# Transposing three more tiles of the last layer on TensorE, adding four residuals on VectorE, with a new order table

## The chip, the core and the metric

The kernel runs on one core of a Trainium2 chip. A core has five engines with a queue each: TensorE (matrix products; PE in the profile, PEld its weight loads), ScalarE (ACT), VectorE (DVE), GpSimd (POOL) and SyncE (SP, which here only issues DMAs). Every engine works its own queue in order, and waits on semaphores for the others. The metric is the device time of one execution, in microseconds; a time for a version is the median of several executions.

## What is computed

A sequence of 2048 tokens with 512 features passes through two layers twice: first a layer A (softmax attention in four segments, with a linear memory carried from one segment to the next), then a layer B (linear attention with softmax feature maps). The weights of both passes are the same. In the text "layer 0" and "layer 1" are the first and the second pass. Layer B matters here:

```python
def _B_ref(x, wqkv, w_phi, wo):
    ...
    phi_q = jnp.concatenate([_softmax(pq, axis=-1), _softmax(-pq, axis=-1)], axis=-1)
    phi_k = jnp.concatenate([_softmax(pk, axis=-1), _softmax(-pk, axis=-1)], axis=-1)
    kv = jnp.einsum('bhsf,bhsd->bhfd', phi_k, v)
    z = jnp.einsum('bhsf->bhf', phi_k)
    num = jnp.einsum('bhqf,bhfd->bhqd', phi_q, kv)
    den = jnp.einsum('bhqf,bhf->bhq', phi_q, z)[..., None] + 1e-06
    o = num / den
    return (lambda x, *d: x.transpose(*d))(o, 0, 2, 1, 3).reshape(B, S, D) @ wo
x = A_x
x = x + _A_ref(_layernorm(x, axis=-1), A_wq, A_wk, A_wv, A_wo, A_beta)
x = x + _B_ref(_layernorm(x, axis=-1), B_wqkv, B_w_phi, B_wo)
x = x + _A_ref(_layernorm(x, axis=-1), A_wq, A_wk, A_wv, A_wo, A_beta)
x = x + _B_ref(_layernorm(x, axis=-1), B_wqkv, B_w_phi, B_wo)
```

`kv` and `z` sum over all tokens, so no query of layer B can be finished before the keys of every token are in. In layer 1 that means: after the last keys, all sixteen query tiles of 128 tokens are finished one after another, and the result is stored.

## The kernel before

**Tiles and stages.** The 2048 tokens are 16 tiles of 128 tokens; four tiles are a segment (layer A) or a query chunk (layer B). The residual stream X stays in on-chip memory for the whole run. Products go to PSUM, which holds four tiles of 1024 columns (slots D0 to D3), shared by everything that TensorE computes: a product must wait until the tile that was last in its slot has been read.

**A query tile of layer B** (`b_query`, from line 1030) goes through these steps. TensorE multiplies the query features by `Rkv` (line 326, called N). For tiles 8 to 15 ScalarE copies this to on-chip memory (line 351, p<-D, 1024 columns). VectorE multiplies by the softmax weights (line 1099). From there two ways lead to the transposed tile oT that the output product needs:

- *by DMA*: VectorE adds the two halves (line 1105), then SyncE issues a DMA transpose (line 364);
- *by TensorE* (keys `("b", L, t)` in `PE_T`): `o_T` lets TensorE multiply both halves by the identity and sum them in PSUM, 16 small products (line 901), then ScalarE or VectorE copies the result out (line 359 or 360). The add of line 1105 falls away, since the sum is made in PSUM.

**The output product** (`out_proj`, line 912; `tproj`; TensorE line 341, D<-WB_o) takes two tiles at once, except for tiles 14 and 15, which go alone (`SOLO`). It is emitted as two halves, each a group of its own in TensorE's queue. The residual is added in one of two ways: for tiles in `RES_PE`, TensorE adds X times the identity to the product (line 341, D<-X,ident) and ScalarE or VectorE copies the sum to X (line 359 or 360); for the others VectorE adds PSUM to X (line 933). In layer 1 a store of the tiles to DRAM follows (line 368, SyncE).

**The order.** The program first lists all 2728 operations with their dependences. A table (`ORDER`, a packed text, read by `place`, line 157) then gives three things: the order in which the operations are emitted, the engine of each, and the buffer slot of each tile. It was made offline by a search. Each engine's queue is the table's order, filtered for that engine, so a queue never overtakes: an instruction whose operands are late holds up everything behind it on its engine. Waits follow from the dependences (`emit`, line 190).

The last part of the queues of the kernel before, unpacked from the table (N13 is the product with `Rkv` of tile 13, T15 the TensorE transpose of tile 15, Wo45a and Wo45b the two halves of the output product of tiles 4 and 5, res the add or copy to X, DT a DMA transpose, st a store):

```
TensorE  Wo89a Wo89b N13 Wo45a N14 Wo45b T15 Wo15a Wo67a Wo15b Wo67b Wo1213a Wo1213b Wo14a Wo14b
ScalarE  copy15 res10/11 Ln Exp copy12 copy13 copy14 evac15 res8/9 res15 res14
VectorE  scale add6 mul12 add12 mul15 mul13 add13 res4/5 mul14 add14 res6/7 res12/13
SyncE    DT4 DT5 st2/3 DT7 DT6 DT12 DT13 st10/11 DT14 st15 st0/1 st4/5 st8/9 st6/7 st12/13 st14
```

Here "scale" is the instruction that completes the softmax weights of tiles 12 to 15 (line 1080).

Of the kernel before, what the change touches and what calls it, by code (L numbers as in the profile page):

```python
# [16 lines left out]
D = 512  # L17
H = 32
# [42 lines left out]
class Tile:  # L61
# [17 lines left out]
    @property  # L79
    def t(self):  # L80
        return self.pool.tensors[self.slot]
# [216 lines left out]
class Kernel:  # L298
# [864 lines left out]
def basep(ap):  # L1163
# [16 lines left out]
        | {("b", 0, t) for t in range(4)} | {("xA", 1, t) for t in range(4)} | {("b", 1, 0), ("b", 1, 15)})  # L1180
RES_PE = {(0, t) for t in (2, 3, 6, 7)} | {(1, t) for t in (2, 3, 6, 7, 8, 9, 10, 11, 12, 13, 14, 15)}
# [8 lines left out]
c-rlE1GHty(q<rit+H*~wr$(CZQHI!vAfVL+cvt(=q?*w|32qd^S%Dxo3-A|nt#^pbMM(ZGb00Ed=dL(d`JKYX#jwsCM1F6Pz!299Y_sHp)OQ{dQcw}6oJan05p__hEN3>K~  # L1190
bm*#h@`Xfu_(5nnMdH4h|AROGpQ;ATJP<f!2@@+CW*z4{f0Yw1aXG586XDC;;i9Jd}hK&;hDLL8t(UAOlo{^H2&pLLo>60`5a6kZ=JET!hYW6>dUyr~xU#LSeWCL*NJK0z;u
2T!OCf6AXjgFdTA1cbEtxAQ{|-QE(Z0z(@#z0r(?igI<sedSMP&0C!+C42GW}JKlwb&>M4N7!1VT&=Vd&9|(uF5Cl2!A$$&5AvLCjT(}OdKzh6ei{Lt>!BEJ6tKcc##(vNSf
5zpo9#+FMTna6)EiQq3Fcu!cBp3tzuqCd6zOW1y!(_Mt{c%3@hqQPHr@(Vu0V^RLK86AC1++uph1edygeUL|^ued_0kYsYScH8sGiJpHI1@7A3&@7~a2V#rj0pG=hT}lUgLg
4E4uV<m8e${jc*u_vU^W!M=g<M;;46rW9dQFZ#EtL_24Ni71YPhGm;v!{Fa|(D9D<9nE5^sZv=ipQP+WpjLGg6xM+tBTj7Gvy_yR{@CwxY&a3n^;r_dQcgQeIS=fZMahTX9n
PJ?++2!F&kv;r&OE@145J@6|ij1_SV7DLTr@oOl88KF3q!ADpW!|@tk$3S?A-#}>`kN2=FmcX}E63gKPjKECrIX*^#Z(tjg!tyvBtKxI2f~&AHRzl?a7>S=^HLQ*+aRy4v44
>ga7>6-%GJb+jP~jAujfWr#*Wx=`gTXKd_kzaQFc&9c4crIoa5PQAF?0iK;#8c5H?bC4%mSO?EzHE2m<N8s)fj}msW!gC?Jx_!g+@3J_d_2VPYdt>%*XXOfr?RM>`%$)3#@~
&a3U3_x;TJt;aCd5NtB$LU_#7Hg=idQp?a8t5~0JUSeSBAZrTl5Nzoq2LD|UQm$;mAlBQ-@A6L+8Y=GS<JLRF~7>I`6U_<Od!MKs$VqV&SOKBrodIup`fHvVKDoD$yBo!f`6
7&o1#22)fijv{?uo;&S@h(hEVYn5($KCh=LvbLLrY)GC^3i*WfI(D>zQV2e4$DvyDoaUeFV>;DlpO0(3LHu)@oTJ4gXtv=Bg@~xH@FQGV`FMWNw6pVLfdf&ML{nbMM<#|IT}
f|s4|Tp<|;ItzQx*9fvQpiYDfW8jw;e*+JiM|AHJdkxR9pM4qQYvs2Y8T)hUpUViRgg)9Dzdq#5)*Or<zfo@P>9I*yK~(Wlgmn$s+Lk8|iG?#IvQ1R`yw*%XgHrxx@T2_~9L
D`_6Jq%Cj?SJ5Xlj$6@bJc#RQJbyulun+g;BX}6s(i%!YLG(3!pi~%4-_sd<P4Ov&=9A=aXf=IF35jVdZJ`acj-u!+eoFy-3?k_$oWoSqkH4dBw4KglZr(u`us^5bowSR>DG  # L1200
!h02<pM3IW_0xG~AN|Ig~n5E-uVLJcc7UjDoockL7}#3?sQHU%^7$i=((0ABGro6+2M@{sBAF7hIf6a&Ioh+4&-t;MVjd58)i#hAyF?0lb@r@<7hZiD(gD#!bAK^Kned&uKX
>l;#N>%4Im5yU=Dn0_k`GwWW!ii8J#c&dTj*I1lDwoSyek7M{W*c`CQ3Fy2eqxF*NobzF=0(Fk78v$z9I<CxHu%JP1i#M8MOAE3%So6E7J$=sbQat1y|F?l9e;Yu8fyU_xUM
Tt2!FXY%%m+SEip2N#{InU)JT%MEi20ln<r~=pL23(s%cq1q0vveA2@FA+hXP~O6&dInT&*Mg1jjQrGn$L~72{+|99G8#NH+-0?iDsOdF3`7pgg)bVoQBfUcbuM1(C7RWU!)
9_k-q2ibdoO7Hm)pA(bv44tB8!8h*$7RZq7$(38$m2oRB}^7QB@6iY?rdSMjI(3$NyUB0d)u9k>;rrYn?!KX5_OnlIB@E+W>j5{1N7YQsBtCwJs`Y(!h`#6OT0@3}Kyqh0(X
32~jQhyf(paiCx!#SJ<O=im(ohy?tWgG70;n=1$uJw<!&!cKrl$z3@U1&ci#B5u)hzD>Qv3$7^k@;<I9_H!lil5308TvF5$uegpVD$ek0E+vYI2I4pz;Oe5ZILk-5jHn?_z)
dPH?$CLzFYeJXE+OtxesP@dQ$0~Ygo?i6C+a66#m`hulocm9O4JoG#6fN<;)#Z$k%%eci*V6Q9OB1xk`MC(dO{H*kvPW>=_#G!<|2+rELw=TBDQ!$3B(1y!U;u75lbW$NyHI
OE|Q7f;v%;aDa2LoBL<6<B9*wrC*c|o5vL$bT;_q|2OcEaigw~Uw--Nh2Qfn2;M}6K$Rmb})FO?z#jV9nZX?o)bfU8CD7uRDqOr&-`ipELyXYjU$Q+`($RKWWPBB1q5k16x?
k0wcJ6u&}6vIR&ahIEj%;FyZ#3RK8F-nXUW5ihTfPdy{@}kHkri)8rhL|a4iOV937$+X`crigN6tl%6o+##sN#Zdt5_833F<Cs}d1AhpBBqK3;uEn|JmqO(iP$EVie=(cv0W
?|&$zl=Ay$f2VyD<3R*N;FhWuP?6zfDy`I%TN){9MIuc)qS$$jEW@rC$GY!)@tF0o(i5PQUK@tycu91v$jP4$har4EYk#UXK4d@Bx%bK<zzB94d?;-okxPK)#6xI8L;5Ld*H
;;J|$>dI^4k+?2S$j73#JSpqR8{)pWDeA~u;<mUWeiEnUT~S{)mS^NWaY~+-PecQGR>p#-;)48HJP^;sMcGg`lIP?r@mjnWO=MH~P+XFiWi#1LR#v}=H=?<`B0q@k@~vngd&  # L1210
_sCis~bK$milmSyh2V*;DqF)zk~oOZJnu<sJD_1WJ-pwv$Tsmn^T!mNG~NOD)^WI!eeNWCwXo)>a`hjx;h<wvu(#Gg(j7R|8~R86kg?*X45=DSwvnWSF#apbVGsrIS(ehD;!
# [72 lines left out]
```

## Time and profile before

| | |
|---|---|
| three runs | 472.95, 474.64 and 475.47 us (median 474.64) |
| the profiled execution, its own time | 472.73 us |
| its span (first to last instruction) | 471.0 us |
| GpSimd busy | 57.4 us (12%) |
| DMA transposes issued by SyncE | 138 (76 p<-p, of attention and query tiles; 54 pX<-p, of normalized tiles; 8 of weights) |
| issue to landing of one, median | 3.0 us (p<-p), 3.3 us (pX<-p) |
| stores of the result | 9, of 256 or 128 KB |
| mean granted TensorE clock | 0.994 of full speed |

How to read the profile: an engine's busy time is the time in which it worked on an instruction. Products are pipelined, so that TensorE's rows overlap and a busy TensorE is not one at its peak. The chain that ended last is followed back from the last instruction: at each step to what released it, or to the instruction before it on its engine. A row of the timeline gives the start, the duration, the engine, the line, the operation with output and inputs, the count, and in brackets the idle time ahead of it with what ended it.

### The profile page before, as it was taken

The numbers are of one execution on the slowest core, as the hardware profiler recorded it, in microseconds if no ns is written. First come the engines' busy times: TensorE is split into PE (matmuls) and PEld (weight loads), VectorE is DVE, ScalarE is ACT, GpSimd is POOL, SyncE is SP. The second block draws the span as 40 slices with busy tenths as digits, with TensorE's granted clock in tenths as the row PEclk, the third lists the DMA queues.
The fourth block names the chain that finished last, engine by engine and source line by source line (L and its number), as shares of the span: only waits on it lengthen the run. The fifth ranks groups of instructions, "written<-read, shape, count | busy, mean of one in ns | idle before, by whom it ended". The sixth has DMA issues, their size and how long they took to land.

```text
span 471.0 us, 25402 instructions
## 1 busy us (share of the span) xinstructions
PE 446.6 (95%) x11753; PEld 299.1 (64%) x11753; DVE 421.5 (90%) x801; ACT 423.8 (90%) x552; POOL 57.4 (12%) x137
## 2 busy tenths in 40 slices
PE   8999899999999999999999999999999999999995
PEld 4566666677667666665556776666677667666552
DVE  6999899999889888989999999998988987998992
ACT  4999999999999997689999999998999999686981
POOL 2312022001011101100420120310110020100000
PEclk9999999999999999999999999999999999999899
DMA  8924534452542031100233454452224104200266
GB/s 256 205 55 76 75 73 99 78 91 27 67 71 43 16 49 31 24 3 14 37 81 59 72 80 55 67 94 48 48 27 61 27 20 65 27 13 3 58 93 191
DMA packets 89388, 30.36 MB, mean 64 GB/s; under 512 B 75954, under 2 KB 89282, under 8 KB 89282
## 3 DMA queue, kind: packets, MB, share of 16 engines
q1 hardware_dynamic: 88450, 28.20, 34.2%
q8 instruction: 92, 1.51, 1.3%
q10 hardware_dynamic: 800, 0.52, 0.4%
q14 instruction: 14, 0.11, 0.1%
q0 software_dynamic: 32, 0.02, 0.0%
HBM read 6.31 MB, written 2.10 MB: 18 GB/s over the span
## 4 chain that ended last, share of the span: by engine, by line
PE 61%; ACT 27%; DVE 6%; DMA 3%; issue 2%; SPq 1%; POOL 0%; DVEq 0%
PE D L341 38%; PE D L326 21%; ACT p L351 15%; ACT pF L351 6%; ACT pE L351 3%; DMA p<-p 2%; PE D L666 2%; DVE X L933 1%; DVE stats L584 1%; ACT pS L351 1%; DMA pX<-p 1%; SPq L364 1%; ACT p L359 1%; ACT X L359 1%; DVE p L878 0%
## 5 line engine op out<-in xcount | busy, mean ns | idle before, releaser
L351 ACT ACTIVATE p<-D 128x1024 bf16<-128x1024 f32 (+1 forms) x224 | 223.0, 1038 | 16.5 <-PE D L341 8.8
L326 PE MATMUL D<-pK,pQ 64*128 64x256 bf16 (+3 forms) x1536 | 115.8, 243 | 5.2 <-ACT pF L351 1.6
L351 ACT ACTIVATE pF<-D 128x896 bf16<-128x896 f32 x128 | 116.8, 939 | 1.8 <-PE D L326 1.5
L326 PEld LDWEIGHTS D<-pK,pQ 64*128 64x128 bf16 x1536 | 55.8, 94 | 43.3 <-ACT p L351 6.3
L326 PE MATMUL D<-pV,pF 64*128 64x34 bf16 x1024 | 75.9, 176 | 1.2 <-ACT pE L351 0.4
L326 PE MATMUL D<-pW,pF 64*128 64x34 bf16 x1024 | 73.3, 176 | 0.0
L592 POOL TENSOR_SCALAR rstd<-mv 128x1 f32<-128x1 f32 x60 | 19.8, 341 | 347.8 <-DVE mv L585 347.5
L326 PEld LDWEIGHTS D<-pV,pF 64*128 64x128 bf16 x1024 | 56.6, 93 | 4.1 <-issue 1.0
L326 PE MATMUL D<-pV,p 64*128 64x34 bf16 x1024 | 53.1, 176 | 1.6 <-issue 1.1
L351 ACT ACTIVATE pE<-D 128x768 bf16<-128x768 f32 x64 | 52.0, 826 | 2.4 <-PE D L326 1.8
L326 PEld LDWEIGHTS D<-pW,pF 64*128 64x128 bf16 x1024 | 53.1, 93 | 1.0
L326 PE MATMUL D<-pW,p 64*128 64x34 bf16 x1024 | 52.1, 176 | 0.0
L326 PEld LDWEIGHTS D<-pV,p 64*128 64x128 bf16 x1024 | 47.2, 93 | 3.6 <-issue 1.2
L326 PEld LDWEIGHTS D<-pW,p 64*128 64x128 bf16 x1024 | 46.0, 93 | 1.4
L326 PE MATMUL D<-tri,two 64*128 64x128 bf16 (+1 forms) x384 | 46.7, 234 | 0.0
L584 DVE BATCH_NORM_STATS2 stats<-X 128x6 f32<-128x512 bf16 x64 | 42.7, 680 | 3.5 <-DMA X<-in_A_x_dram 3.2
L326 PE MATMUL D<-pV,pE 64*128 64x34 bf16 x512 | 45.1, 175 | 0.0
L326 PE MATMUL D<-pW,pE 64*128 64x34 bf16 x512 | 43.2, 175 | 0.0
L980 DVE TENSOR_REDUCE pS<-p 128x64 f32<-128x1024 bf16 (+1 forms) x36 | 38.7, 1092 | 1.2 <-ACT p L351 1.2
L341 PE MATMUL D<-pX,WA_q 64*128 64x512 bf16 x256 | 37.6, 376 | 0.3 <-issue 0.2
L341 PE MATMUL D<-pX,WA_k 64*128 64x512 bf16 x256 | 37.0, 376 | 0.5 <-DVE stats L584 0.5
L341 PE MATMUL D<-WB_k,pX 64*128 64x512 bf16 (+1 forms) x288 | 33.8, 353 | 2.2 <-issue 1.4
(135 smaller groups left out, 998.5 us busy)
## 6 DMA issues: line engine op xcount, KB each, us to landing
pW<-pV SPq DMA_DIRECT2D x16, 136.0 KB, 2.8
out_dram<-X SPq DMA_DIRECT2D x7, 256.0 KB, 2.7
X<-in_A_x_dram SPq DMA_DIRECT2D x3, 512.0 KB, 7.4
pX<-in_B_wqkv_dram SPq DMA_DIRECT2D x3, 512.0 KB, 4.9
p<-p SPq DMA_TRANSPOSE x76, 3.0
pX<-p SPq DMA_TRANSPOSE x54, 3.3
WA_k<-in_A_wk_dram SPq DMA_DIRECT2D x2, 256.0 KB, 6.5
WA_v<-in_A_wv_dram SPq DMA_DIRECT2D x1, 512.0 KB, 8.2
```

Of the source, the lines that this page charges most:

```text
L326: ins = e.matmul(out_ap, lhsT, rhs, start=st, stop=sp, tile_position=(basep(lhsT), basep(out_ap)))
L341: ins = e.matmul(out_ap, lhsT[64 * hf:64 * hf + 64], rhs[64 * hf:64 * hf + 64], start=k == 0 and i == 0, stop=k == 1 and i == len(lists[hf ...
L351: return self.g.op({"act": (dur, lambda e: e.activation(out_ap(), in_ap(), func, scale=scale))}, reads, writes, opens, label=label)
L359: ch = {"act": (n / 1.2 + 51, lambda e: e.activation(out_ap(), in_ap(), ACT.Copy)), "dve": ((340 if fast else n / 0.96 + 65), lambda e: e. ...
L364: return self.g.op({"sp": (1200.0, lambda e: [e.dma_start(out_ap(), in_ap(), transpose=True)])}, reads, writes, opens, kind="d", lat=1450. ...
L584: v(lambda e: e.bn_stats(self.stats[:, t, :], self.X[:, t, :]), 602, [R("X", t)], [R("st", t)], label="bn")
L592: v(lambda e: e.tensor_scalar(rs, self.mv[:, t, 1:2], LN_EPS, None, op0=ALU.add), 170, [R("mv", t)], [R("rstd", t)], eng="pool", label="rstd")
L666: ins = e.matmul(D.t[c0:, r0 * 8:r0 * 8 + n], r[:, c0:], ones(r, n), start=True, stop=True, tile_position=(r0, c0))
L933: self.v(lambda e: e.tensor_tensor(X(), X(), src(), ALU.add), 65 + 512 * n / 0.96, pr + xr, xr, label="res")
L980: fn = lambda e, sgn=sgn, eo=eo, Z=Z, n=n: e.tensor_reduce(Z.t[:, 0:64 * n].rearrange("p (k s h) -> p k s h", k=n, s=2)[:, :, sgn, :], eo( ...
```

## The change

Three sets and the table change; no line of the program does.

```diff
 PE_T = ({("xA", 0, t) for t in range(4)} | {("xB", L, 15) for L in range(2)} | {("a", L, 3, 2, 1) for L in range(2)}
-        | {("b", 0, t) for t in range(4)} | {("xA", 1, t) for t in range(4)} | {("b", 1, 0), ("b", 1, 15)})
-RES_PE = {(0, t) for t in (2, 3, 6, 7)} | {(1, t) for t in (2, 3, 6, 7, 8, 9, 10, 11, 12, 13, 14, 15)}
+        | {("b", 0, t) for t in range(4)} | {("xA", 1, t) for t in range(4)} | {("b", 1, 0)} | {("b", 1, t) for t in (12, 13, 14, 15)})
+RES_PE = {(0, t) for t in (2, 3, 6, 7)} | {(1, t) for t in (2, 3, 6, 7, 8, 9, 10, 11)}
...
 ORDER = """
-c-rlE1GHty(q<rit+H*~wr$(CZQHI!vAfVL+cvt(=q?*w|32qd^S%Dxo3-A|nt#^pbMM(ZGb00Ed=dL(d`JKYX#jwsCM1F6Pz!299Y_sHp)OQ{dQcw}6oJan05p__hEN3>K~
...
+c-rlHWt1I9vSvVXbGKT|%*@Qp%*@Qp%*@Qp!k1XNCq*3EoQJKTWCw#s@ocm?Xlm^JNtg@?Af}vZ&qeSMtl+RMV!iW8Xz4Yq=({A2dY9jNDg(O1XP21P#+X9q=J&r0IEYG(9
...
```

- Tiles 12, 13 and 14 of layer 1 are transposed by TensorE, as tile 15 already was: three adds (line 1105) and three DMA transposes go, three groups of 16 small products (line 901) and three copies out of PSUM come, two on VectorE (tiles 12 and 14) and one on ScalarE (tile 13).
- The residuals of tiles 12 to 15 of layer 1 are added by VectorE (line 933) in place of TensorE's product with the identity and a copy: tiles 12 and 13 in one instruction, 14 and 15 in one each.
- The table is replaced as a whole. The search that made the new one let transposes be issued and land late at random. Both tables hold the same 2728 operations (six of them in their new form). Unpacked, the new table is a local re-sorting of the old one: on TensorE 583 of 1054 operations stand at another rank in the queue, by 14 ranks at most; on ScalarE 230 of 547, by 5 at most; on SyncE 129 of 184, by 33 at most; on VectorE 607 of 792, by up to 73. Twelve operations beside the six move to another engine.

The same part of the queues in the new table:

```
TensorE  Wo89a N12 Wo89b N14 T15 Wo45a T12 Wo45b T13 Wo15a T14 Wo15b Wo1213a Wo67a Wo1213b Wo67b Wo14a Wo14b
ScalarE  copy15 res10/11 Ln Exp copy13 copy12 evac15 copy14 res8/9 evac13 res6/7
VectorE  scale mul15 add6 mul12 mul13 evac12 mul14 evac14 res4/5 res15 res12/13 res14
SyncE    DT4 DT5 st10/11 DT7 DT6 st0/1 st4/5 st8/9 st2/3 st15 st12/13 st6/7 st14
```

Its PSUM slots there: D0 holds N13, T15, T12, Wo15 in turn; D1 N12, Wo45, Wo14; D2 N14, T13, Wo1213; D3 Wo89, T14, Wo67.

In the middle of the run the largest moves are on VectorE. Around 86 to 113 us and 274 to 313 us of the profile before, instructions that prepare later tiles move forward in its queue by 12 to 32 ranks: four of the normalization's statistics (line 584), six single-input operations of layer A's feature map (lines 642 and 643) and four normalizations (line 605).

More of the change, by code (lines that the diff above doesn't have):

```diff
@@ L1194 @@
[L1194 to L1201, printed above, removed]
@@ new lines @@
+jT4KqE*DjiEd=fl|;E3IIVfXbvr)CA0zut)Vm|0Sj%QEwqCQAfY`7=m0gKBBX|lP!KvoCny9VP!lpi8K?w>p)-_)TF?d3LJ_D8wV?`hg?tbON#Oz%g;00^SD+ZAgv{^|x<Pl
+i1wG&@42PUB0(!zD7zx+lHY9{8&<jSxSV#lcVHDhe$1nyi!eG1vcOVPo!rTxEccC}@0DWOG41*}hjX7W-<iRD-5Bk6m><=5@CTxLRuoNysU(AbnAsoJgJn$3VgYhs9(qTW`3
+LBw4ZiDog3Gd(l_z^ZiYwUpELuQ-`1F;PPZ-)Dj6_&vY7zERxBd&r$xEhwj6POMe@F^^U39ubjLML2;8SyRj$H6cMeu8(f6lcIATmygua3b8r4<I{c#RD)B3t|?$hdFQ*7Qk
+$n6Nf-N{28CaBp3=WAwPD;xsVShLm`Zhg)splK7$Wo2Mk36U2rFK$6<*4Gc3awFb{g*T3C)V;W5sF`xpcXF#?8TBJ7C+Xf}+&#5e*6(r9dpub~Kz#rg0IyJ9<B2f^?Iu7}TI
@@ new lines @@
+1$M)g_%pqNUbqUg!E-E%NwGKf!3CgrHIBoDP!e}TF^mV}u`-rIV#X@?8N`B*pg2yzkD&yX$4IPzlduf_h-I-Hmd45WnzBPh+z&4>3U|RTR0*%)6P$(Buqr0O*%%8qV0GMxHL
+xbG!}VAT*I)*aNVpcK;X$~L-+)4awebN?$8X^fyu@gnhg<O}YJ7+{a5El;aTJ8}aSKktI%v`0CorC-;tY&~H&Jt4oQZRA0saE@a4z<vg?J0Uf=Lt`zlPh`pC;2LT#O~D6fMF
+*R3B5)Hr$R)u>lUI2^1fuP+V+=&2b{7qF-SurKW~hl(Lb-?39;^Q9k+t8lj?9^d;n=+|&YBQ%?E-L$EO#&O@4BVSZ|fxu_QzdX2#tiaTf`G8dp$Xz4@TNxkV8TtO>o2NouvU
+nvZC;xl@OyRZnAp*>ifnqX=A43|*}`W%PQ8z@KNxSYz;ZcIj>!bgbo1r{WtLbMl$QgSL!^(g`mVFhYHsjwkErxcVL)8H^_MEh_A4X0%IF@Ay-DTtbp<)$=}l4BoAfuG_S+K*
@@ L1246 @@
+b0Iw*9!b9^ob@zLcJt$n4dXcl}{0`Xi-ssM*h)NMTGgrFg&K-y(D|t!hrr5XzaNXaMxe<8Bb&dhIn~ao*RL_$^jyv$6y(N<zWo6%7X>$=gU8V`h9{UDLi1r%L-{3<YN%zwS)
+i{{gZW|v|@UvH~4I#z#RorAbgF69Ymqea|pbVvQKsI<Q{kz@^%M@d#w#3{MrvF^WcVfc@chI{9Jh+doD%A#MQ5O<E7R5P2Gd8ypVbP1FvL^_wnm0$g9zCjZSg2#t_epMG93U
+V|ng)ZOfAK3ZAuJzM-)If~Dsg8WF@C9B8}|)@v+Y_!WZJa4Eu*#bAJFi1HwXP>>g~Ft#4H{{{M(iBt
 """
```

93 lines of the change are left out of this document (45 added, 48 removed).

## The prediction

> **What bounds the kernel now.** I read the page first, then the busy times by stretch, then the chain and the timeline of the last 30 us.
>
> ```profile
> span 471.0 us, 25402 instructions
> ...
> PE 446.6 (95%) x11753; PEld 299.1 (64%) x11753; DVE 421.5 (90%) x801; ACT 423.8 (90%) x552; POOL 57.4 (12%) x137
> ...
> PE 61%; ACT 27%; DVE 6%; DMA 3%; issue 2%; SPq 1%; POOL 0%; DVEq 0%
> ```
>
> Three engines are near full, and the chain runs over TensorE and ScalarE; DMA and SyncE's queue hold 4% of it. The shares are means over stages, so the stretches come next (columns: length, then busy time of PE, PEld, DVE, ACT, POOL, granted clock, DMA share, GB/s).
>
> ```profile
> 100.00:140.00 40.00, 38.42 (x1132) 27.85 (x1124) 35.54 (x62) 37.88 (x46) 4.03 (x8) 1.00 0.46 63
> 260.00:300.00 40.00, 38.99 (x1156) 27.70 (x1148) 38.00 (x76) 39.32 (x48) 8.77 (x20) 1.00 0.48 70
> 457.90:463.10 5.20, 3.66 (x57) 1.99 (x49) 3.05 (x4) 2.31 (x4) 0.00 (x0) 1.00 0.39 71
> 463.10:467.30 4.20, 3.95 (x40) 1.69 (x40) 1.64 (x2) 0.05 (x1) 0.00 (x0) 1.00 0.86 248
> 467.30:471.00 3.70, 0.00 (x0) 0.00 (x0) 0.00 (x0) 0.55 (x1) 0.00 (x0) 0.74 0.74 250
> ```
>
> In the middle ScalarE and TensorE have almost nothing left: 0.68 us idle of 40 on ScalarE from 260 on. The tail is different: from 457.9 on no engine is full, and from 467.3 on only the last copy and the stores remain. The chain names what holds it.
>
> ```profile
> 457.94 0.59 DVE X L933
> 458.53 4.06 DMA p<-p
> 462.59 0.53 issue
> 463.12 1.27 PE D L341 x10
> ...
> 467.25 0.60 ACT X L359
> ```
>
> A DMA transpose of 4.06 us, then four halves of output products, then one copy. The transpose waits in SyncE's queue, the products of tiles 12 and 13 wait for it, and that of 14 follows.
>
> **The tail, part by part.** These rows of the timeline carry the costs.
>
> ```profile
> 442.03 0.69 DVE L360 CAST p<-D 128x512 bf16<-128x512 f32 x1
> ...
> 453.35 0.65 ACT L351 ACTIVATE pS<-pS 128x128 f32<-128x128 f32 x2
> ...
> 455.08 6.85 SPq L364 DMA_TRANSPOSE p<-p  x4
> ...
> 456.86 1.04 PE L341 MATMUL D<-WB_o,p 64*128 64x512 bf16 x8
> 457.07 1.02 ACT L351 ACTIVATE p<-D 128x1024 bf16<-128x1024 f32 x1 [0.51 <-PE D L326]
> 457.73 0.41 PE L901 MATMUL D<-ident,p 64*128 64x64 bf16 x16
> 458.17 0.60 ACT L359 ACTIVATE p<-D 128x512 bf16<-128x512 f32 x1
> 459.08 0.68 DVE L1099 TENSOR_TENSOR p<-p,pS 128x1024 bf16<-128x1024 bf16 x1
> 459.80 0.42 DVE L1105 TENSOR_TENSOR p<-p 128x512 bf16<-128x512 bf16 x1
> 460.57 0.60 PE L341 MATMUL D<-WB_o,p 64*128 64x256 bf16 x8
> 462.94 1.19 SPq L364 DMA_TRANSPOSE p<-p  x1
> 463.12 0.39 PE L341 MATMUL D<-X,ident 64*128 64x512 bf16 x2 [0.87 <-DMA p<-p]
> 463.34 1.04 PE L341 MATMUL D<-WB_o,p 64*128 64x512 bf16 x8
> 464.19 4.16 SPq L368 DMA_DIRECT2D out_dram<-X  x7
> 465.70 0.28 PE L341 MATMUL D<-X,ident 64*128 64x256 bf16 x2
> ```
>
> *Removed:* on VectorE three adds of 0.42 us; on SyncE three transposes, of 1.19 us of issue each (one here alone; four in a row took 6.85); on TensorE the identity products of the residuals, which make 1.26 us of a half (463.12 to 464.38) where 1.04 is enough without, and add some 0.1 to the 0.60 of a lone tile's half. *Added:* on TensorE three transposes of 0.41 us; on VectorE two copies of 0.69, on ScalarE one of 0.60. *Exchanged:* VectorE's residual adds cost what its copies did for two tiles; for one tile the row is
>
> ```profile
> L933 DVE TENSOR_TENSOR X<-X,D 128x512 bf16<-128x512 bf16 x6 | 4.0, 683 | 0.4 <-PE D L341 0.4
> ```
>
> against ScalarE's 0.60. For one tile the way from the multiply to oT was 0.42 for the add, 1.19 of issue and a landing 3 us after it; it becomes 0.41 and 0.60 to 0.69. But the new chain passes through PSUM slots and through VectorE's queue, so I follow it through the new table's queues instead of subtracting. I start both from the same point: ScalarE ends its last Exp of the weights at 454.00 (453.35 and 0.65); up to there the two tables issue the same ScalarE and VectorE work.
>
> 1. ScalarE: copy13, copy12, evac15, copy14: three copies of 1.02 and one of 0.60, 3.66 us at most, some 0.1 less at each overlap of neighbours. copy14 ends about 457.45.
> 2. VectorE: mul12 needs copy12 (ends 455.9): 455.95 to 456.65 (0.68); mul13 to 457.3. TensorE's T12 needs slot D0, which evac15 frees at 456.5; it ends about 457.25. So evac12 runs to 458.05 and mul14 to 458.75.
> 3. T14 (slot D3, free once res8/9 has ended at 458.45) runs 458.85 to 459.25; evac14, 0.69, ends at 460.0. What is behind evac14 in VectorE's queue (res4/5, res15) is not urgent yet, except that Wo14 needs the slot of Wo45, freed by res4/5 at 461.2, before its turn comes.
> 4. Wo67 uses T14's slot, so it cannot start ahead of 460.05. From there stand five halves: 1.26, 1.04, 1.26, 0.60, 0.60. End to end they make 4.76; in groups that interleave, starts stand closer by the product's last 0.16 (457.73 lies 0.17 before the end of 456.86 and 1.04), 4.1. I take 4.6, since each half waits for its first. The last ends at 464.65.
> 5. VectorE adds tile 14, 0.68: 465.4. Before, the last copy ended at 467.85 (467.25 and 0.60).
>
> From there to the end of the span before is 3.15 us (issue and landing of the last store); I leave it. Ahead of it SyncE issues seven stores behind res4/5 (461.2), as many as the seven that took 4.16 us before from 464.19; they begin 3 us earlier, so they don't bind. The tail gains 467.85 - 465.4 = **2.45 us**. Bounds: if all engines had to work end to end and VectorE's two evacuations came a product (1.04) late, 1.0; if the evacuations don't hold the slots and Wo67 starts with T13 done (458.9), 3.6.
>
> **The rest of the table.** The new order is a local re-sorting, so stages stay where they are. The waits of TensorE that it could remove are few:
>
> ```profile
> PE D L341 <- issue: 1.9, 3, 1.4
> PE D L341 <- DMA p<-p: 1.5, 2, 0.9
> ...
> PE D L341 <- DMA pX<-p: 0.5, 1, 0.5
> ```
>
> The 0.9 belongs to the tail. The others, 0.6 and 0.5, and the 1.4 of "issue", ahead of a product whose operand is a late normalized tile, make 2.5 us, the most that earlier transposes give directly. The other bound is a loss through VectorE's new order (below). Transposes that are ready sooner stand ahead of others in SyncE's queue at the place of the 0.5; at the others little changes. I take a gain of 0.5.
>
> **Sum.** 472.73 - 2.45 - 0.5 = 469.8 for an execution like the profiled one. That one was the fastest of the four known; their mean is 473.95, 1.2 above it, the median of the three runs 1.9 above. I add 1.2 here and to each rival: **471.0 us**, its own range 468.5 to 473.5.
>
> **Rival 1: the gain is eaten by a slow clock.** The granted clock fell once ahead of the tail:
>
> ```profile
> 434.00:436.00 2.00, 1.30 (x50) 1.05 (x52) 1.82 (x6) 1.56 (x4) 0.00 (x0) 0.74 0.00 0
> 436.00:438.00 2.00, 2.00 (x37) 1.06 (x35) 2.00 (x4) 1.83 (x4) 0.00 (x0) 0.50 0.04 8
> 438.00:440.00 2.00, 2.00 (x88) 1.55 (x84) 1.56 (x5) 1.66 (x2) 0.00 (x0) 0.91 0.32 66
> ...
> 435.75 1.91 PE L341 MATMUL D<-pX,WB_q 64*128 64x512 bf16 x8
> ```
>
> Eight products took 1.91 us instead of 1.04 there, behind a stretch of many small products and waits. The lost clock is 2 times (0.26 + 0.50 + 0.09), 1.7 us of full-speed work. The new tail has such a stretch from 455.3 to 459.5: four transposes of 64 columns, with waits for copies between them. A dip behind it would fall on the last halves: 469.8 + 1.7 + 1.2 = 472.7, and with the slots' lower bound (1.0 instead of 2.45) 474.2; I name 473.6. Against it: from 457.9 to 463.1 TensorE was busy 3.66 of 5.20 us, and its clock stayed at 1.00.
>
> The Trainium skill, "TensorE: Matmul & The Clock Gate", Part 1, has a rule for it: the array runs at half clock after a window of about 3.4 us without enough activity and at full clock after a busy one, with windows that run freely. The rows agree with half clock (0.50) and about its length; by this rule the dip before may vanish or move in any execution, which is no reason to expect it more after.
>
> **Rival 2: the whole order gains.** The 2.5 us of waits go, and what stood behind them moves up: 472.73 - 2.45 - 2.5 + 1.2 = 469.0. For it: DMA and SPq are 4% of the chain. Against it: TensorE was busy with other work during most of those links.
>
> **Rival 3: slower, by VectorE's order.** Place: layer 0 at 86 to 113 us and layer 1 at 274 to 313, where the new table brings preparations for later tiles ahead of evacuations that TensorE's slots and ScalarE's inputs wait for. The rows:
>
> ```profile
> L584 DVE BATCH_NORM_STATS2 stats<-X 128x6 f32<-128x512 bf16 x64 | 42.7, 680 | 3.5 <-DMA X<-in_A_x_dram 3.2
> ...
> L605 DVE TENSOR_SCALAR p<-X,mv,rstd 128x512 bf16<-128x512 bf16 x64 | 24.6, 400 | 0.6 <-POOL rstd L594 0.5
> ...
> L642 DVE TENSOR_SCALAR p<-pK 128x1024 bf16<-128x1024 bf16 x12 | 5.0, 419 | 0.0
> ```
>
> Price: 4 x 0.68 + 4 x 0.40 + 6 x 0.42 = 6.8 us, if none is absorbed: 472.73 - 2.45 + 6.8 + 1.2 = 478.3. It decides from 5.3 us on, where it outweighs 2.45 + 0.5 by the 2.4 us that make half a per cent. For it: VectorE has 2.0 us idle of 40 from 260 on, ScalarE 0.68. Against it: from 100 to 140 VectorE has 4.5 us idle, and other instructions move back by as much, so that most evacuations keep their rank.
>
> **That the change doesn't do what it says** (a table made against random lateness that meets the chip's lateness no better) is inside the forecast: it rests on the tail alone.
>
> **How the numbers follow.** Half a per cent, 2.4 us, is about what a measurement of this kernel can tell from no change; it puts the borders at 472.3 and 477.0. The forecast has 0.50 (0.42 faster, 0.08 same), rival 1 0.20 (0.01, 0.18, 0.01), rival 2 0.12 (all faster), rival 3 0.18 (0.00, 0.03, 0.15). Together: faster 0.55, same 0.29, slower 0.16. The range: down to rival 2 with the tail's better bound and without the 1.2 (469.0 - 1.15 - 1.2 = 466.6), up to rival 3's price, 478.3.
>
> **What would show it.** Right: VectorE's last row is a residual add of 128x512 that ends 5 to 6 us before the span's end; no DMA p<-p in the last 12 us of the chain; TensorE's idle time between the last Exp of the weights and its own last product falls below 2 us. Step 3 is wrong if T14 starts well after mul14's end. Rival 1 shows as a granted clock under 0.9 in the last 12 us, rival 3 as ScalarE busy less than 37.5 of 40 us around 100 to 140 or 260 to 300 with VectorE as releaser. The forecast fails if the stretch up to that Exp (454.00 us before) changes by more than 2.5 us.

## The result, and the profile after

The changed kernel took 469.21 us in the median of four executions (468.53 to 471.16), the kernel before 475.06 us beside it: a ratio of 0.989, 95% interval 0.984 to 0.994. Twelve more executions, taken later beside 27 of the kernel before, gave 0.993 (0.990 to 0.996). The first ratio makes the gain 5.3 us (3.0 to 7.5), the second 3.4 us (1.9 to 4.8). The profiled execution took 468.75 us, its span 466.7 us (472.73 and 471.0 before).

The page of the profile of the kernel after gives the span, the busy times, the shares of the chain, and the median landing of query and attention transposes.

```profile
span 466.7 us, 25467 instructions
...
PE 446.3 (96%) x11789; PEld 298.7 (64%) x11789; DVE 420.2 (90%) x800; ACT 423.3 (91%) x552; POOL 56.2 (12%) x138
...
PE 57%; ACT 34%; DVE 4%; DMA 3%; issue 2%; POOL 1%; SPq 0%; DVEq 0%
...
p<-p SPq DMA_TRANSPOSE x73, 3.1
```

The engines do as much work as before (TensorE 446.6 us then, 446.3 now) in a span that is 4.3 us shorter, so what went is waiting. The two stretches in the middle, in the columns of the windows shown before:

```profile
100.00:140.00 40.00, 38.39 (x1142) 27.45 (x1138) 35.25 (x63) 38.58 (x47) 2.98 (x8) 1.00 0.27 46
260.00:300.00 40.00, 38.85 (x1200) 28.06 (x1196) 37.90 (x76) 39.14 (x48) 7.40 (x17) 1.00 0.46 70
```

ScalarE stays at 38.6 and 39.1 of 40 us: it is not starved by VectorE's new order, and rival 3 is out. The rows of the tail, from the timeline:

```profile
451.66 0.66 ACT L351 ACTIVATE pS<-pS 128x128 f32<-128x128 f32 x2
451.80 0.69 SPq L368 DMA_DIRECT2D out_dram<-X  x1
...
455.11 1.04 PE L341 MATMUL D<-WB_o,p 64*128 64x512 bf16 x8 [0.92 <-DMA p<-p]
...
455.97 0.41 PE L901 MATMUL D<-ident,p 64*128 64x64 bf16 x16
...
456.43 0.69 DVE L360 CAST p<-D 128x512 bf16<-128x512 f32 x1 [0.96 <-PE D L901]
...
457.03 0.68 DVE L1099 TENSOR_TENSOR p<-p,pS 128x1024 bf16<-128x1024 bf16 x1
...
457.77 0.41 PE L901 MATMUL D<-ident,p 64*128 64x64 bf16 x16
...
458.22 0.69 DVE L360 CAST p<-D 128x512 bf16<-128x512 f32 x1 [0.51 <-PE D L901]
...
461.47 1.22 DVE L933 TENSOR_TENSOR X<-X,D 128x1024 bf16<-128x1024 bf16 x1 [0.83 <-PE D L341]
...
463.66 0.69 DVE L933 TENSOR_TENSOR X<-X,D 128x512 bf16<-128x512 bf16 x1 [0.97 <-PE D L341]
```

The last Exp of the weights ends at 452.32 (454.00 before), the last residual at 464.35 (467.85), the span at 466.7 (471.0). So by these two executions 1.7 us were gained ahead of the tail, 1.8 in it, and 0.8 behind the last residual. The chain of waits says what the new tail waits for:

```profile
446.12 1.83 ACT p L351 x2
449.62 5.41 DMA p<-p
455.11 1.04 PE D L341 x8
458.18 4.78 PE D L341 x52
```

The transposes of tiles 12 to 14 have left the chain, and an older one stands in it, that of tile 5: 5.41 us from its issue to the product that needs it, for which TensorE idles 0.92 us. The transpose of tile 12 by TensorE (455.97) stands behind that product in the queue.

Were these three pieces the change's doing? Two traces can't tell. The experiments take the pieces apart, and each leaves a further trace of a part of the old or the new order.

### The profile page after: what moved, and what is told of

The parts are those of the page before. It is cut to its first block, busy times and chain, and to the rows that moved or that the text cites. A ratio compares the mean times of both kernels' runs of the same rounds, so it can differ in the third digit from the quotient of the medians.

```text
span 466.7 us, 25467 instructions
## 1 busy us (share of the span) xinstructions
PE 446.3 (96%) x11789; PEld 298.7 (64%) x11789; DVE 420.2 (90%) x800; ACT 423.3 (91%) x552; POOL 56.2 (12%) x138
## 4 chain that ended last, share of the span: by engine, by line
PE 57%; ACT 34%; DVE 4%; DMA 3%; issue 2%; POOL 1%; SPq 0%; DVEq 0%
PE D L341 36%; PE D L326 18%; ACT p L351 18%; ACT pF L351 9%; ACT pE L351 4%; DMA p<-p 2%; PE D L666 2%; DMA pX<-p 1%; ACT pS L351 1%; DVE X L933 1%; ACT p L359 1%; DVE p L795 1%; DVE pK L360 0%; POOL rstd L594 0%; ACT X L359 0%
## 5 line engine op out<-in xcount | busy, mean ns | idle before, releaser
L326 PE MATMUL D<-pK,pQ 64*128 64x256 bf16 (+3 forms) x1536 | 114.2, 243 | 5.1 <-ACT p L351 1.3
L592 POOL TENSOR_SCALAR rstd<-mv 128x1 f32<-128x1 f32 x60 | 16.2, 275 | 351.8 <-DVE mv L585 351.7
L980 DVE TENSOR_REDUCE pS<-p 128x64 f32<-128x1024 bf16 (+1 forms) x36 | 38.6, 1090 | 0.3 <-ACT p L351 0.2
L594 POOL TENSOR_TENSOR rstd<-rstd,mhalf 128x1 f32<-128x1 f32 x60 | 37.9, 639 | 2.4
L933 DVE TENSOR_TENSOR X<-X,D 128x1024 bf16<-128x1024 bf16 (+1 forms) x30 | 32.1, 1074 | 6.4 <-PE D L341 6.2
```

Of the source, the lines that this page charges most:

```text
L326: ins = e.matmul(out_ap, lhsT, rhs, start=st, stop=sp, tile_position=(basep(lhsT), basep(out_ap)))
L592: v(lambda e: e.tensor_scalar(rs, self.mv[:, t, 1:2], LN_EPS, None, op0=ALU.add), 170, [R("mv", t)], [R("rstd", t)], eng="pool", label="rstd")
L594: v(lambda e: e.tensor_tensor(rs, rs, self.mhalf[:], ALU.pow), 540, [R("rstd", t), R("mhalf")], [R("rstd", t)], eng="pool", label="rstd")
L933: self.v(lambda e: e.tensor_tensor(X(), X(), src(), ALU.add), 65 + 512 * n / 0.96, pr + xr, xr, label="res")
L980: fn = lambda e, sgn=sgn, eo=eo, Z=Z, n=n: e.tensor_reduce(Z.t[:, 0:64 * n].rearrange("p (k s h) -> p k s h", k=n, s=2)[:, :, sgn, :], eo( ...
```

## The experiments

### The tail alone, and the rest of the table alone

The two tables agree on the set of operations that come first at several places, so they can be cut there: at position 2655 of 2728 (about 450 us), and at position 1300 (about 216 us). Each part keeps its own order, engines and buffers.

```diff
 tail_only
-order = new[0:2655] + new[2655:2728]
+order = old[0:2655] + new[2655:2728]
 bulk_only
-order = old[0:2655] + old[2655:2728]
+order = new[0:2655] + old[2655:2728]
```

> The first 2655 of the 2728 instructions in the order, engines and buffers of the kernel before, the last 73 (from 450 us on) in those of the kernel after, with its three TensorE transposes and its VectorE residual adds. The tail's term of the prediction (2.45 us): 2.45 us below the kernel before. What the two traces show of the tail (1.8 us up to the last residual add, 0.8 us from there to the end): 1.8 to 2.6 us below it. The rival, that the gain came from the rest of the table: within 0.5 us of the kernel before.

> The other half of the same cut: the first 2655 instructions as in the kernel after, the last 73 as in the kernel before (three DMA transposes, residuals of tiles 12 to 15 by TensorE). The prediction's term for the rest of the table: 0.5 us below the kernel before. What the two traces show at the last Exp of the weights: 1.7 us below it, and up to 3 us if the clock dips as briefly as in the trace of before (3.4 us instead of 6.8 us at half clock). The rival, that the table's body is worth nothing and the traces differ by the clock alone: within 0.4 us.

The tail alone: 471.47 us, ratio to before 0.9935 (0.9907 to 0.9963), which is 3.1 us (1.8 to 4.4). The rest alone: 472.88 us, ratio 0.9969 (0.9941 to 0.9996), 1.5 us (0.2 to 2.8). So by the middle values the tail carries two thirds of the gain, and the two rivals "nothing from the tail" and "nothing from the rest" fall, the second narrowly. tail_only holds the new forms and the new order of the last 73 operations together; of these the residuals alone are taken apart below, so what the three transposes give without the new order is not measured. The tail in tail_only:

```profile
454.43 0.64 ACT L351 ACTIVATE pS<-pS 128x128 f32<-128x128 f32 x2
...
457.04 1.04 PE L341 MATMUL D<-WB_o,p 64*128 64x512 bf16 x8 [0.23 <-ACT p L351]
...
460.14 0.69 DVE L360 CAST p<-D 128x512 bf16<-128x512 f32 x1 [0.51 <-PE D L901]
...
465.58 0.69 DVE L933 TENSOR_TENSOR X<-X,D 128x512 bf16<-128x512 bf16 x1 [0.97 <-PE D L341]
```

From the end of the Exp (455.07) to the last residual (466.27) it takes 11.20 us, 0.8 less than the same operations in the kernel after: the wait at tile 5 is 0.23 us here instead of 0.92.

### The two halves of the rest

```diff
 first_half
+order = new[0:1300] + old[1300:2728]
 second_half
+order = old[0:1300] + new[1300:2655] + old[2655:2728]
```

> The first 1300 instructions (to 216 us) in the order of the kernel after, the rest as in the kernel before. From two traces of the old body (before, tail_only) and four of the new one (after, bulk_only, res_pe, store_behind), all in one execution each: at 216 us the new one stands at 0.6 to 1.8 us, mean 1.1, ahead of the trace of before, but 0.3 more ahead of tail_only. If the new order gains there: 1 to 1.4 us below the kernel before. If the executions differ by chance alone: within 0.4 us.

> The middle part, instructions 1301 to 2655 (216 to 450 us), in the order of the kernel after, the first 1300 and the last 73 as in the kernel before. In the six traces the middle part up to 415 us is 0.7 to 1.3 us shorter in the new order than in before and tail_only, and the clock's dip then takes back 0.4 to 0.8 us (6.8 us at half clock in all four of the new order, 3.4 us in both of the old): 0.2 to 0.9 us below the kernel before. If the dip costs what the clock record says, half of 3.4 us more: 0.5 us above it.

first_half took 473.33 us, ratio 0.9989 (0.9956 to 1.0021); second_half 472.83 us, ratio 0.9973 (0.9944 to 1.0001). What the rest of the table gives, it gives after 216 us, some 1.3 us, at the edge of what can be told from nothing; the 1 to 1.4 us that the traces promised for the first half did not come. The traces side by side show how far one of them can mislead, in us from the span's start (the end of the first 2473 of the 2728 operations, the same set in both orders; the end of the Exp; and, as the tail, the time from there to the last residual):

```
                order up to 450 / tail   first 2473   Exp's end   tail
before          old / old                  415.4       454.0      13.85
tail_only       old / new                  415.7       455.1      11.20
after           new / new                  412.4       452.3      12.03
after_again     new / new                  414.6       454.8      12.01
bulk_only       new / old                  413.8       453.9      12.98
res_pe          new / new, residuals       413.9       453.9      13.00
store_behind    new / new, store moved     413.8       453.5      11.69
```

after_again is the kernel after, run again; it and the last two are told of below. One body of operations, run five times, ends its first 2473 anywhere from 412.4 to 414.6. The trace of after was the most fortunate of them. The means (415.5 old, 413.7 new) differ by 1.9 us; at the end of the Exp 0.9 of it is left (454.5 and 453.7). The section on the clock shows where the rest goes. The old tail takes 12.6 to 13.9 us in four traces (second_half 12.60, first_half 13.72, and two above), the new one 11.2 to 12.0 in four (without res_pe): 1.6 us between the means, just below the interval of the times (1.8 to 4.4).

The pieces behind the last residual go by chance and not by the tail: from it to the span's end stand 3.1 us in before, 3.4 in first_half and 2.3 in bulk_only with the old tail, 2.4 in after, 2.6 in tail_only and 3.7 in fill_light (below) with the new one.

### The residuals put back on TensorE

```diff
-RES_PE = {...} | {(1, t) for t in (2, 3, 6, 7, 8, 9, 10, 11)}
+RES_PE = {...} | {(1, t) for t in (2, 3, 6, 7, 8, 9, 10, 11, 12, 13, 14, 15)}
```

> The kernel after with the residuals of tiles 12 to 15 of layer B put back on TensorE as products with the identity; their last step is a copy on the same engine at the same place of the order. If TensorE sets the end of the tail, each of the four tiles costs it 0.21 us (distance from the first identity product to the first product that follows it, 448.12 to 448.33 in the trace of after): 0.85 us above the kernel after. If the chain of VectorE and ScalarE sets the end: within 0.3 us of it.

The time was 471.48 us, ratio to before 0.9936 (0.9913 to 0.9959), against 0.9929 (0.9899 to 0.9959) for the kernel after: too close for the times to settle 0.85 us. The trace does it by rows (the last one is the copy that stands in the place of the VectorE add):

```profile
459.01 0.27 PE L341 MATMUL D<-X,ident 64*128 64x256 bf16 x2
459.12 0.60 PE L341 MATMUL D<-WB_o,p 64*128 64x256 bf16 x8
...
463.58 0.38 PE L341 MATMUL D<-X,ident 64*128 64x512 bf16 x2
...
463.80 1.03 PE L341 MATMUL D<-WB_o,p 64*128 64x512 bf16 x8
...
466.20 0.69 DVE L360 CAST X<-D 128x512 bf16<-128x512 f32 x1 [1.19 <-PE D L341]
```

Each identity product of a lone tile's half pushes the next product back by 0.11 us (459.01 to 459.12), that of a pair's half by 0.22; four and two of them make 0.88 us. The tail is 13.00 us instead of 12.03, 0.97 more, of which 0.12 is the wait at tile 5 (1.04 instead of 0.92). From there on TensorE sets the end of the new tail, and by these rows the residual adds are worth their 0.85 us: about half of the 1.6 us that the rows show for the tail, a quarter of the 3.1 us of the times.

### The store moved behind the transposes

```diff
-SyncE  DT4 DT5 st10/11 DT7 DT6 st0/1 ...
+SyncE  DT4 DT5 DT7 DT6 st10/11 st0/1 ...
```

> The kernel after with one store (tiles 10 and 11) moved in SyncE's queue from between the transposes of tiles 5 and 7 to behind that of tile 6. If the store's traffic slows the transpose of tile 5 (5.4 us from issue to landing, where the transposes of its kind have a median of 3.1): that landing falls to 3 to 4 us, TensorE's wait of 0.92 us at 455.1 goes, and the end comes 0.4 to 0.9 us earlier (transposing tile 12 then waits for VectorE's product, which ends 0.5 us before it is transposed now). If the transpose is late by itself: the wait stays at 0.9 us and the time within 0.3 us of the kernel after.

The time was 470.77 us, ratio 0.9915 (0.9884 to 0.9946). TensorE's wait at tile 5 came to 0.59 us, neither 0 nor 0.9, and the landing to 5.1 us; with the store in its old place it had been 5.4 (after), 5.4 (after_again), 5.5 (res_pe) and 4.1 (tail_only). In the three kernels with filling, below, TensorE's wait is 0.1 us (and ends with ScalarE, not with the transpose), with the store in its old place (two) and moved (one). The store is at most a small part of what makes it late. Narrow windows of the DMA view of the kernel after, from tile 5's issue at 449.62 on, show another part (columns of a queue: packets, MB, share of the 16 DMA engines' time; of an issue: median landing):

```profile
q1 hardware_dynamic: 533, 0.13, 48.6%
q8 instruction: 1, 0.02, 7.3%
...
p<-p SPq DMA_TRANSPOSE x1, 5.4
...
q1 hardware_dynamic: 494, 0.12, 78.2%
q14 instruction: 1, 0.01, 5.3%
```

The two windows lie at 449.6 to 450.9 and 450.9 to 452.9. In each starts one packet of a queue that the profile names "instruction": it takes 7.3% of 16 x 1.3, 1.5 us, and 5.3% of 16 x 2.0, 1.7 us. The packets of tile 5's transpose follow these two. Of its 512 packets of 256 bytes 472 have started by 451.6; none starts then until 452.1, when the first instruction packet ends (450.59 to 452.11), and 34 go one after another; the last six start from 453.18 on, when the second ends (451.50 to 453.19). So a part of the transpose waits behind each. The landing at 455.02 still comes 1.6 us behind its last packet, where that of tile 7 comes 0.5 us behind; this part is not explained. Over the records of eight traces, transposes counted by how many such packets (8 or 16 KB) overlap the time from 0.3 to 2.4 us behind their issue:

```
packets   transposes   issue to landing, us: 10%   median   90%
   0          285                            2.41    2.45   2.67
   1          727                            2.43    3.45   4.27
   2           62                            2.98    4.06   4.74
```

So the lateness of a transpose goes with these packets. That they load the program itself is read from the queue's name. The table is a relation in records and not an experiment: moving the loads was not tried.

### Every transpose made late

The new table was searched with transposes that issue and land late. If that made it tolerant, the kernels should move apart when all transposes are late.

```diff
 late_before, late_after (def tr)
-[e.dma_start(out_ap(), in_ap(), transpose=True)]
+[e.dma_start(self.scr[...], self.inp["A_beta"][None, 0:2]), e.dma_start(out_ap(), in_ap(), transpose=True)]
```

> The kernel before with every one of its 138 DMA transposes made late: once its input is ready, SyncE first issues a load of 4 bytes into a cell that nothing reads, then the transpose, and the consumer waits for both. With a delay of 0.65 us each (the issue of one plain transfer on SyncE in the tail takes 0.4 to 0.7 us) the transposes whose time from issue to first use leaves less than that over a landing of 3.1 us add up to 3.2 us in the trace of before, with 1 us to 6.9 us. Both theories: 2 to 8 us above the kernel before.

> The same delay in front of each of the 135 DMA transposes of the kernel after. If the new order tolerates late transposes better: by the same sum 1.6 us (delay of 0.65 us) or 4.6 us (1 us), so it loses 1.6 to 2.3 us less than the kernel before loses, and the distance between the two grows from some 4.5 to 6 to 7 us. The rival, that the orders are equally tolerant and the difference is the tail's: both lose the same within 0.7 us.

late_before took 493.1 us, ratio to before 1.039 (1.034 to 1.044), late_after 486.1 us, ratio to before 1.025 (1.020 to 1.030). Both lose much more than expected, 18.4 us (3.87% of 474.7) and 15.6 (2.48% and the 0.81% by which after lies below before, its two ratios weighted by executions). SyncE's queue in late_after points at why:

```profile
457.00 0.42 SPq L365 DMA_DIRECT2D scr<-in_A_beta_dram  x1
457.47 1.81 SPq L366 DMA_TRANSPOSE p<-p  x1
459.38 0.36 SPq L365 DMA_DIRECT2D scr<-in_A_beta_dram  x1
459.79 1.19 SPq L366 DMA_TRANSPOSE p<-p  x1
```

Each small load takes 0.41 to 0.47 us of the queue up to the next transpose, and the transposes come in groups, so the delays of a group add up; the sum over single slacks left that out, which would explain the miss. The distance between the two came to 7.0 us (some 3 us to either side by the two intervals), and the traces tell where it lies. At the Exp's end late_before stands at 474.2 and late_after at 471.7: 2.5 us apart, 19.6 and 18.0 us behind the means of their bodies. The rest lies in the tail, 15.65 us in late_before and 11.20 in late_after. With nearly equal losses up to the Exp (at the end of the first 1300 operations late_after even stood 10.7 us behind the trace of before, late_before 6.1), a greater tolerance of the table's body is not shown. The tail is more tolerant: late_before's is 1.8 us longer than the longest undelayed one, with TensorE idle four times for 3.8 us together, and late_after's is as short as tail_only's, without three of the late links.

### The clock

All seven traces of the list above show a stretch at half clock ahead of the tail. In the kernel after (length, then busy time of PE, PEld, DVE, ACT, POOL, granted clock, DMA share, GB/s):

```profile
430.00:432.00 2.00, 1.46 (x90) 1.35 (x92) 1.23 (x6) 1.56 (x5) 0.00 (x0) 0.91 0.05 8
432.00:434.00 2.00, 1.38 (x62) 1.13 (x56) 1.97 (x3) 1.15 (x3) 0.00 (x0) 0.50 0.00 0
434.00:436.00 2.00, 1.54 (x75) 1.54 (x77) 1.62 (x6) 2.00 (x5) 0.00 (x0) 0.50 0.12 24
436.00:438.00 2.00, 2.00 (x22) 0.61 (x16) 2.00 (x7) 2.00 (x4) 0.00 (x0) 0.50 0.45 92
438.00:440.00 2.00, 1.93 (x32) 0.94 (x32) 2.00 (x6) 1.18 (x6) 0.00 (x0) 0.88 0.55 97
```

The clock lost is 2 x (0.09 + 0.50 + 0.50 + 0.50 + 0.12) = 3.4 us, so 6.8 us at half speed; in before it was 3.4 us long. The other four traces of the new body have 6.8 us too, tail_only with the old one has 3.4; second_half, new from 216 us on, has 6.8, and first_half, old there, none. The executions that left no trace agree: the mean granted clock is 0.990 over bulk_only's and 0.994 over those of the kernel before beside it. Here the 1.9 us of the body shrink to 0.9: from the first 2473 operations to the Exp's end the two traces of the old body need 38.6 and 39.4 us, the five of the new 39.7 to 40.3. The test is to give TensorE work there; the edit is that of fill_light.

```diff
+FILL = {(1, 0, 0, 1): 2, (1, 2, 1, 1): 4, (1, 1, 1, 1): 6}
...
-for tt in range(4) for gg in range(2) for hf in range(2)],
+for tt in range(4) for gg in range(2) for hf in range(2)] +
+[(ZQ.t[:, hf * 512 + 256:hf * 512 + 512], self.ident[64 * hf:64 * hf + 64, :], self.WB["q"][64 * hf:64 * hf + 64, 0, 0:256], True, True)
+ for _ in range(FILL.get((L, c, gp, sgn), 0)) for hf in range(2)],
```

> The kernel after, unchanged, for a comparison on the chip of the next two runs and a further execution of its trace. By the two halves measured apart (ratio 0.9935 for the tail, 0.9969 for the rest) the whole stands at 0.990; by the first four executions at 0.989. If those four were favoured by chance: 0.992 or above.

> The kernel after with 12 pairs of products added on TensorE (64 rows, 256 columns, 0.107 us a pair; they write PSUM columns that nothing reads) where it idles between small products in layer B's last part: 2 pairs ahead of the idle 0.27 us at 430.1, 4 ahead of 0.41 us at 431.5, 6 ahead of 0.72 us at 434.4. They lie in idle time, so by themselves they cost 0 to 0.2 us. If the clock dips because TensorE does little work there: one of the two stretches of 3.4 us at half clock goes, or both, and the time falls by 0.5 to 1.5 us against the kernel after. If the dip comes whatever TensorE does: 6.8 us at half clock as in all five traces of this body, and 0 to 0.5 us slower.

> The same with 30 pairs (3.2 us of TensorE work, beside all twelve groups of small products), of which about 1.6 us fits into idle time. If the dip follows the amount of work: both stretches at half clock go, which gives 1.0 to 1.5 us, and up to 1.6 us of added work takes that back: within 0.6 us of the kernel after, with a clock record at 1.0 from 420 to 445 us. If the dip comes whatever TensorE does: 1.5 to 3 us slower, with 6.8 us at half clock.

> fill_light and store_behind together: the 12 pairs of products in idle time and the store of tiles 10 and 11 behind the transpose of tile 6. If both gains hold, 1.2 us (the means of fill_light and after_again, 470.06 and 471.27) and 0.3 us (TensorE's wait at tile 5, 0.92 us in after, 0.59 us in store_behind): a ratio of 0.987 to 0.990 to the kernel before, and no clock below full speed between 420 and 445 us in the trace. If fill_light's gain was chance: 0.992 to 0.993, as after_again. If the store has nothing to do with tile 5's landing, TensorE's wait there lies anywhere from 0.2 to 1.0 us, as in the traces with and without the move so far.

The same windows in fill_heavy:

```profile
430.00:432.00 2.00, 1.99 (x92) 1.77 (x88) 1.12 (x4) 1.50 (x3) 0.00 (x0) 1.00 0.00 0
432.00:434.00 2.00, 1.50 (x74) 1.34 (x75) 1.31 (x4) 1.46 (x3) 0.00 (x0) 1.00 0.04 8
434.00:436.00 2.00, 1.62 (x74) 1.36 (x68) 1.97 (x4) 1.50 (x4) 0.00 (x0) 1.00 0.00 0
436.00:438.00 2.00, 1.78 (x58) 1.13 (x58) 2.00 (x8) 1.46 (x3) 0.00 (x0) 1.00 0.41 86
```

The dip is gone in all three filled traces, and the mean granted clock over the executions goes from 0.991 (after_again) to 0.996 (fill_light) and 0.999 (fill_heavy): the dip follows the work.

The 14 traces tell which measure of work (a product's columns are the last number of its shape: 512 in 64x512). All lengths in their clock records, but for the last one of a trace, are whole multiples of 3.413 us (3.41, 6.83, 27.3, 211.6 and 430.1 among them). On the grid of that step, 17 windows at full clock are followed by half clock; TensorE was busy 17 to 87% of them, with products of 1,152 to 6,672 columns in all. Of the 1,864 that kept full clock some were busy only 50%, and all but 12 had more columns than that, the 12 from 5,504 on. Half clock went on behind windows of 3,200 to 6,400 columns and ended behind 6,528 or more. So the columns decide, with a border at some 5,500 to 6,700, and not the busy time. The long dip has two such windows in a row, in after with 4,032 and 3,488 columns; before has 3,200 and then 6,848.

The times gain little. after_again: 471.09 us, ratio 0.9929 (0.9899 to 0.9959), which by what was expected means that the first four executions were favoured by chance, though 0.990 lies inside the interval; fill_light 469.99, 0.9898 (0.9864 to 0.9932); fill_heavy 471.14, 0.992 (0.9891 to 0.9948), its added products having eaten what the clock gave. fill_store, with the light filling and the moved store, came to 472.16, 0.9939 (0.9913 to 0.9966), above both ranges expected, and its executions had clocks from 0.988 to 0.998. The light filling leaves windows of 5,816 (fill_store) and 6,912 columns (fill_light), at the border, so it may keep the clock up only in some executions; the heavy one leaves none under 9,088. The mean clock can't show this by itself, for it counts other places: fill_light's own trace has 0.994 without a dip ahead of the tail, from 3.4 us at half clock near 216 us (tail_only and first_half have that one too) and 2.4 us behind TensorE's last product. So fill_light's gain over the kernel after, 1.1 us of median, did not come back, and no version here is shown to beat the kernel after. Over some 210 executions of these kernels (without the late ones), a line with a level for each puts the price at 0.39 us (standard error 0.07) for each us of lost clock, so that the longer dip, 1.7 us of lost clock more, costs an estimated 0.7 us of the 1.0 us that the stretch is longer. The traces without a dip bear it out: from the first 2473 operations to the Exp's end fill_light and fill_store need 39.3 and 39.1 us where the five of the new body need 40.0 in the mean (fill_heavy, with its added products, 40.6).

## Why the prediction was right

**The place and the size.** The forecast had the tail as what gains, by 2.45 us, and the rest of the table by 0.5. Measured apart they are 3.1 us (1.8 to 4.4) and 1.5 us (0.2 to 2.8); the tail's term lies inside its interval, the other inside but near its edge. The forecast was 471.0 us; the two samples have medians of 469.21 and 471.09. That the second lies so near is in part luck: as a gain over the mean of 473.95 from which it started the forecast was 2.95 us, and the two samples have 5.9 and 3.6 between their medians.

**The tail, step by step.** The 2.45 us took the old tail from one trace, whose 13.85 us are the longest of four (13.3 in the mean); the rows of all traces make the gain 1.6 us. Steps 1 to 5 make 11.4 us from the end of the Exp to that of the last add (465.4 - 454.0). tail_only and all three filled kernels took 11.20, within 0.2. The kernel after took 12.03, and the step that failed there is the second: the transpose of tile 12 was to wait for its slot and end 3.25 us behind the Exp (mul12's end at 456.65 and the 0.41 of a transpose make 3.06). It ended 4.06 behind it (456.38), since the first half of tiles 4 and 5 stands ahead of it in TensorE's queue and waited 0.92 us for tile 5's DMA transpose. The prediction followed VectorE's and ScalarE's queues through the tail, and took the DMA transposes that remained as landed. Step 3 held: the transpose of tile 14 starts at 457.77, right behind VectorE's product for it (457.03 and 0.68), and its copy ends at 458.91, 6.6 behind the Exp where 6.0 were worked out; the difference comes from step 2.

**Behind the last residual** the prediction left 3.15 us unchanged. The 0.8 us that after's trace shows less lie within the scatter of 2.2 to 3.7 us over all traces, old and new tails alike.

**The rest of the table** was the mis-sized term: 0.5 taken, 1.5 measured. In the traces the new body is 1.9 us ahead at 415 us, and half of that goes in the longer dip, which leaves 0.9. That the waits removed are those that the prediction listed (2.5 us in its rival 2) is not shown: up to there TensorE's idle time ended by a DMA falls from 1.3 us (two traces of the old body) to 0.6 (five of the new), and that ended by VectorE, which the prediction feared would grow, from 4.0 to 3.1. The latter falls in first_half too (2.7), whose time hardly moved. So the cause of this part stays open.

**Rival 1** had the right mechanism in the wrong place. The new tail never dipped while TensorE worked, but the dip ahead of it grew from 3.4 to 6.8 us. The prediction looked for new small products only from 455 us on, and not at how the new order places those of the query chunks ahead. In before, windows of 2 us with many products lie at 432 to 436 us (128 and 50, with 42 and 28 in the two ahead of them); in after at 428 to 436 (72, 90, 62 and 75). **Rival 3** did not occur: ScalarE's busy time in its two stretches is 38.6 and 39.1 us, above the 37.5 that would have shown it.

**The marks.** Two of the signs did not come. VectorE's last row is a residual add of 128x512, but it ends 2.35 us before the span's end and not 5 to 6: the 5.6 us (471.0 - 465.4) were counted to the end of the span before, which was to move as well. And a DMA transpose p<-p does reach into the chain's last 12 us, tile 5's (449.62 to 455.03 of 466.7), where none was to stand. The others came: TensorE's idle time behind the Exp was 0.92 us and nothing else above 0.1, under the 2 us named. The stretch up to the Exp changed by 1.7 us, under the 2.5 that would have ended the forecast.

## What to carry to other kernels

When a link is taken off the end of a chain, look at once for the next late operand in the same queue, here an older transpose that nobody had waited for; it decides how much of the gain arrives. A pair of traces of two versions holds a microsecond or two of chance at every milestone, so cut the change in two and measure the parts, and lay the traces of equal parts beside each other, before giving a piece of the difference a cause. Gathering small products into one longer stretch can cost clock: in these traces it took back half of what the new order had gained ahead of it.

## What the runs showed of the hardware

- **DMA transposes are late where packets of the queue "instruction" run.** In the 466.7 us of the kernel after, of 25,467 instructions, 92 such packets of 16 KB and some of 8 KB run, those of 16 KB for about 1.1 us each (1.4% of 16 x 466.7 us, over 92). A transpose that meets none lands in 2.45 us, one that meets two in 4.06 (medians), and at tile 5 in 5.4. This is a relation; only for tile 5 was it followed packet by packet, and there some 1.1 us of the landing stay unexplained.
- **A busy TensorE can lose its clock.** In the kernel after it was busy 2.7 of the 3.4 us from 428.2 on and never idle for more than 0.41 us in a row, mostly with products of 8 and 64 columns, and was set to half speed at 431.65; 30 pairs of products of 256 columns among these kept it at full speed. Over 14 traces the columns of a window of 3.41 us decide, with a border at some 5,500 to 6,700, at full clock and at half. The Trainium skill, "TensorE: Matmul & The Clock Gate", "Why this matters for your kernels", advises against idle gaps of more than about 3 us between bursts to keep the clock. These rows show a loss without any such gap, so that rule isn't sufficient here. The lengths, 3.4 and 6.8 us, agree with the window of about 3.4 us of its Part 1.
